# A two-layer kernel (beacon attention, then a squared-ReLU MLP): planner costs taken from landing times, and zero matmuls in TensorE's early gaps

## The chip, the cores and the metric

The kernel runs on one NeuronCore of a Trainium2 chip. The metric is the device time of one execution in microseconds (us), as a median over several executions. The engines are TensorE (PE), VectorE (DVE), ScalarE (ACT), GpSimd (POOL) and SyncE (SP); each works through its own list of instructions in order, and semaphores hold an instruction until what it needs is there. SP only issues transfers (DMA); ACT and POOL issue some as well.

## The reference

Eight batches of eight heads with 576 tokens and 64 features per head attend causally to their own keys and to 16 beacon keys that stand ahead of them. The result, 4608 tokens by 512 features, goes through two matrices with a squared ReLU between them. Inputs and output are float32.

```python
def _attn_ref(q, k, v, beacon_k, beacon_v) -> np.ndarray:
    B, H, S, D = q.shape
    scale = 1.0 / np.sqrt(D)
    k_all = np.concatenate([beacon_k, k], axis=2)
    v_all = np.concatenate([beacon_v, v], axis=2)
    Nb = beacon_k.shape[2]
    scores = scale * np.matmul(q, k_all.transpose(0, 1, 3, 2))
    causal = np.zeros((S, Nb + S), dtype=bool)
    causal[:, Nb:] = np.triu(np.ones((S, S), dtype=bool), k=1)
    scores = np.where(causal, -1000000000.0, scores)
    scores = scores - scores.max(-1, keepdims=True)
    a = np.exp(scores)
    a /= a.sum(-1, keepdims=True) + 1e-09
    return np.matmul(a, v_all).astype(np.float32)

def _moe_ref(x, w_in, w_out) -> np.ndarray:
    h = x @ w_in
    r = np.maximum(h, 0.0)
    g = r * r
    return (g @ w_out).astype(np.float32)
```

## The kernel before

Work is cut into small named pieces (`Op`), and a planner (`Order.run`) writes down the order in which each engine gets them. It plays the run forward with a cost for each piece: when an engine is free it takes, of the pieces whose needs are met, the one of lowest `prio`. The order it finds is then emitted, and the real engines follow it, each in its own order, with real waits. So a cost changes nothing but the order.

A load has two costs in the plan. `dur` is how long its engine is busy issuing it, and `dma` is added to one common time `dma_free`, so that loads share one line of transfers; the planner counts the data as there 1.6 us after that. Loads on one queue go at most 4 (SP) or 8 (ACT, POOL) deep.

The stages of a batch b (heads in four pairs; pair p = 4b + pr):

- Loads. Batch 0's q and k come through `add_first_loads` (`fld`, tokens 0 to 239, into the output staging buffers `osb`, cast by DVE and ACT) and `add_part_loads` (`sld`, tokens 240 to 575, cast on the way by POOL's transfers). Batch 1's q and k come by `sld` alone. From batch 2 on each of q, k, v is loaded in five chunks of up to 128 tokens (`add_load`, `ld`) into one of eight staging buffers `stg`, and POOL casts each chunk to bf16 (`cast`, line 299, by the helper `copy_on`). The fifth chunk has 80 rows for k and v. v of batches 0 and 1 is loaded by POOL, all else of `ld` by SP. The weights w_in and w_out come in four quarters each, from POOL; batch 2's first load waits for the last quarter of w_out.
- Transposing q and k: on PE for batches 0 and 1 (`tp`, lines 451 and 454, evicted by DVE or ACT), by two DMA transposes on SP from batch 2 on (`tr`, line 376). The beacon keys are loaded apart (`bkl`), cast by DVE (`bkc`) and transposed on PE (`tpb`).
- Scores (`qk`, line 589) into one of two PSUM strips, the exponential on ACT (`exp`, line 604) into one of four buffers `pt`, a causal mask on DVE (`mask`), then `av` on PE (line 639). From batch 1 on av p.0.0 and av p.0.1 are the two heads of a pair; each has 15 matmuls, and the last needs the fifth v chunk. DVE divides by the sums (`norm`), and the result is transposed into xT, on PE for batches 0 to 2 (`xtp`), by five DMA transposes on SP after that (`xt`, line 690).
- The MLP runs in nine chunks of 512 tokens: s1.j.f (line 770) multiplies chunk j with w_in, ACT or DVE apply the ReLU, DVE squares, s2.j.t.q (line 805) multiplies with w_out in quarters; ACT or DVE copy to `osb`, SP stores (`st`).

The MLP of one chunk is spread between the pieces of the next batches' attention; after the last batch it runs alone.

The memory that a piece uses is checked by the framework, which adds the waits. The costs of a load stand here; a cast is due once its load counts as there:

```python
        ld = add(f"ld{b}{x}{c}", "POOL" if soft else "SP", 1.3 if lo else 0.65, emit_load,
                 prio=prio, take=("stg", "stg"), dma=(1.15 if b < NPE else 1.25) * rows / 128, behind=load_chain[-1:] + behind, sync=sync)
```

Of the kernel before, what the change touches and what calls it, by code (L numbers as in the profile page):

```python
# [16 lines left out]
class Op:  # L17
# [1 line left out]

    __slots__ = ("name", "engs", "dur", "emit", "prio", "need", "users", "left", "ready",  # L20
                 "take", "give", "gate", "held", "slots", "dma", "pe_time", "behind", "followers",
                 "sync", "insts")

    def __init__(self, name, engs, dur, emit, prio=0.0, deps=(), take=None, give=None,
                 gate=None, dma=0.0, pe_time=0.0, behind=(), sync=()):
        self.name = name
        self.engs = engs if isinstance(engs, (tuple, list)) else (engs,)
        self.dur = dur
        self.emit = emit
        self.prio = prio  # L30
        self.sync = list(sync)
        self.need = list(deps) + self.sync
        self.users = []
        self.take = (*take, 1)[:3] if take else None
        self.give = give
        self.gate = gate
        self.held = None
        self.slots = []
        self.dma = dma
        self.pe_time = pe_time  # L40
        self.behind = list(behind)
        self.followers = []


class Order:
# [2 lines left out]

    LAT = {"PE": 0.2, "ACT": 0.2, "DVE": 0.15, "POOL": 0.25, "SP": 0.1, "-": 0.0}

    DEPTH = {"SP": 4, "ACT": 8, "POOL": 8}
    DMA_LAT = {"SP": 0.6, "ACT": 0.6, "POOL": 2.0}

# [7 lines left out]
    def add(self, *a, **kw):  # L61
        op = Op(*a, **kw)
        op.need = [d for d in op.need if d is not None]
        self.ops.append(op)
        return op

    def run(self):
# [16 lines left out]
        free = {e: 2.3 if e == "DVE" else 0.0 for e in engines}  # L84
        dma_free = 0.0
        lanes = {"SP": [], "POOL": [], "ACT": []}
        events = [(0.0, 0, None, None)]
        seq = 0
        started = set()
        issued = []  # L90
        now = 0.0
        while events:
            now = events[0][0]
            while events and events[0][0] <= now + 1e-9:
                _, _, kind, op = heapq.heappop(events)
                if kind == "done":
                    for u in op.users:
                        u.left -= 1
                        if u.left == 0:
                            release(u)  # L100
                elif kind == "give":
                    from_op, which = op.give if isinstance(op.give, tuple) else (op.give, 0)
                    pool, cls = from_op.take[:2]
                    self.pools[pool].append(from_op.slots[which])
                    if cls in self.inuse:
                        self.inuse[cls] -= 1
            again = True
            while again:
                again = False
                for e in engines:  # L110
                    if free[e] > now + 1e-9:
                        continue
                    best = None
                    fallback = None
                    for op in avail[e]:
                        if any(free[x] <= now + 1e-9 for x in op.engs[:op.engs.index(e)]):
                            continue
                        if op.take:
                            pool, cls, need = op.take
                            if len(self.pools[pool]) < need:  # L120
                                continue
                            if cls in self.limits and self.inuse[cls] + need > self.limits[cls]:
                                continue
                        if op.gate is not None and not op.gate(self):
                            if fallback is None or op.prio < fallback.prio:
                                fallback = op
                            continue
                        if op.dma and len(lanes[e]) >= self.DEPTH[e] and lanes[e][-self.DEPTH[e]] > now + 1e-9:
                            continue
                        if best is None or op.prio < best.prio:  # L130
                            best = op
                    if best is None:
                        best = fallback
                    if best is None:
                        continue
                    op = best
                    started.add(id(op))
                    for u in op.followers:
                        u.left -= 1
                        if u.left == 0:  # L140
                            release(u)
                    for ee in op.engs:
                        avail[ee].remove(op)
                    if op.take:
                        pool, cls, need = op.take
                        op.slots = [self.pools[pool].pop(0) for _ in range(need)]
                        op.held = (pool, cls, op.slots[0])
                        if cls in self.inuse:
                            self.inuse[cls] += need
                    dur = op.dur[e] if isinstance(op.dur, dict) else op.dur  # L150
                    end = now + dur
                    free[e] = end
                    self.progress += op.pe_time
                    issued.append((op, e, now))
                    seq += 1
                    heapq.heappush(events, (end, seq, "free", op))
                    if op.dma:
                        dma_free = max(dma_free, now + self.DMA_LAT[e]) + op.dma
                        seen = max(end, dma_free + 1.6)
                        lanes[e].append(seen)  # L160
                        seq += 1
                        heapq.heappush(events, (seen, seq, "free", op))
                    else:
                        seen = end + self.LAT[e]
                    seq += 1
                    heapq.heappush(events, (seen, seq, "done", op))
                    if op.give is not None:
                        seq += 1
                        heapq.heappush(events, (seen, seq, "give", op))
                    again = True  # L170
        assert len(issued) == len(self.ops), [o.name for o in self.ops if id(o) not in started][:20]
        for op, e, _ in issued:
            if e != "-":
                op.insts = op.emit(e)
# [8 lines left out]
def kernel(  # L183
# [11 lines left out]
    nc = tc.nc  # L195
    B, H, S, D = q.shape
    Nb = beacon_k.shape[2]
    HP = H // 2
# [69 lines left out]
        limits={"av": 2, "tp": 2},  # L268
    )
    order.wait_for = wait_for  # L270
    add = order.add

    nc.vector.memset(warm, 0.0)
    for i in range(2):
        nc.vector.memset(kT[i][:, :, Nb + S:NT * 128], 0.0)
        nc.vector.memset(vb[i][:, :, :, D:D + 1], 1.0)
    for p in pt:
        nc.vector.memset(p[:, :, 928:1952].rearrange("p h (a w) -> p h a w", w=512)[:, :, :, 0:96], 0.0)
        nc.vector.memset(p[:, :, 1824:2048], 0.0)

# [47 lines left out]
    def add_load(b, x, c, prio, behind=[], sync=[]):  # L328
# [10 lines left out]
        def emit_load(e):  # L339
            st = stg[ld.held[2]]  # L340
            insts = []
            if lo:
# [3 lines left out]
            return insts  # L346

        ld = add(f"ld{b}{x}{c}", "POOL" if soft else "SP", 1.3 if lo else 0.65, emit_load,
                 prio=prio, take=("stg", "stg"), dma=(1.15 if b < NPE else 1.25) * rows / 128, behind=load_chain[-1:] + behind, sync=sync)
        load_chain.append(ld)  # L350

        def emit_cast(e):
# [19 lines left out]
    def add_trans(b, x, prio):  # L372
        srcb, dst = (qb, qT) if x == "q" else (kb, kT)

        def emit(e):
            nc.sync.dma_start(
                out=dst[b % 2].rearrange("p g (c t) -> p (g c) t", c=NT),
                in_=srcb[b % 2].rearrange("p g c d -> p (g c d)"),
                transpose=True,
            )  # L380

        deps = [cast[b, x, c] for c in range(NT)]
        deps += [o for p in range(HP * (b - 2), HP * (b - 1)) for o in qk_ops[p]]
        trans[b, x] = [add(f"tr{b}{x}", "SP", 4.1, emit, prio=prio, deps=deps, dma=4.5)]

    def add_beacon(b, prio):
        prio = prio if b else -299.5
# [3 lines left out]
        bk = add(f"bkc{b}", "DVE", 0.4, lambda e: nc.vector.tensor_copy(bks[b % 2], bkf[b % 2]), prio=prio,  # L391
                 deps=[ld])
        cast[b, "bk"] = bk
        box = {}

        def emit_tp(e):
# [15 lines left out]
    def add_part_loads(b, part, prio, after, free, sync=()):  # L412
        t0, np_, ns = parts_of[b][part]
        step = HP // 2
        for pr in range(0, HP, step):
            h = slice(2 * pr, 2 * (pr + step))
            for n, (x, t) in enumerate((("k", k), ("q", q))):
                def emit(e, t=t, x=x, h=h):
# [1 line left out]
                        out=strided_buf(b, x, part)[:, h],  # L420
                        in_=t[b, h, t0:t0 + np_ * ns, :].rearrange("h (p s) d -> p h s d", s=ns))]
                o = add(f"sld{b}{x}{part}.{pr}", "POOL", 0.75, emit, prio=prio + pr + 0.1 * n, behind=after,
                        sync=() if pr or n else sync, deps=free, dma=1.07 if b == 0 else 1.5)
                after = [o]
                for i in range(step):
                    strided[b, part, pr + i, x] = o
# [2 lines left out]
    def add_strided(b, prio):  # L429
# [6 lines left out]
        for part, (t0, np_, ns) in enumerate(parts_of[b]):  # L436
            n_tok = np_ * ns
            for pr in range(HP):
# [3 lines left out]
                for n, xs in enumerate(groups):  # L442
                    box = {}

                    def emit_tp(e, xs=xs, pr=pr, box=box, part=part, np_=np_, ns=ns, n_tok=n_tok):
                        pp = ps[box["t"].held[2]].bitcast(BF16)
                        for i, x in enumerate(xs):
                            for u in range(ns):
# [5 lines left out]
                                    nc.tensor.transpose(pp[64 * hj:64 * hj + 64, at:at + np_],  # L454
                                                        strided_buf(b, x, part)[:, 2 * pr + hj, u, :], ident[0:np_, 0:np_])

                    tp = add(f"tp{b}.{part}.{pr}{xs}", "PE", 0.1 + (0.1 if b == 0 else 0.075) * ns * len(xs), emit_tp,
                             prio=100.0 * (HP * b + pr) - (190 if b else 90) + 0.1 * n + 1000.0 * part,
                             deps=[strided[b, part, pr, x] for x in xs] + [ident_op] + busy, take=("ps", "tp"))
                    box["t"] = tp  # L460
# [16 lines left out]
    def add_first_loads():  # L477
# [4 lines left out]
        for lo, hi in ((0, 1), (1, 2), (2, HP)):  # L482
            for n, (x, t) in enumerate((("k", k), ("q", q))):
# [4 lines left out]
                        out=raw[n][:, h],  # L488
                        in_=t[0, h, t0:t0 + np_ * ns, :].rearrange("h (p s) d -> p h s d", s=ns))]

                o = add(f"fld{x}{lo}", ("SP", "ACT")[n], (0.45, 0.55)[n], emit, prio=-300.0 + lo, dma=0.68 * (hi - lo))
                first.append(o)
                for pr in range(lo, hi):
                    def emit_cast(e, x=x, n=n, pr=pr):
# [425 lines left out]
```

The softmax here doesn't subtract the row's maximum and nothing guards it: scores larger than these inputs give would overflow.

## Time and profile before

| | |
|---|---|
| time, median of 9 runs | 345.82 us (344.93 to 346.82) |
| the profiled execution | 345.45 us, span from first to last instruction 343.7 us |
| TensorE busy | 330.5 us (96%) |
| ScalarE busy | 194.6 us (57%) |
| VectorE busy | 168.3 us (49%) |
| GpSimd busy | 89.5 us (26%) |
| first matmul | at 3.89 us |
| last quarter of w_out landed, SP's first load of batch 2 | 49.2 us |
| granted TensorE clock in the page's row of slices | 9 (90% or more) in all |

A row of the timeline gives start, length, engine, line, operation, output and input, partitions x elements, and how many instructions were merged into it; in square brackets stand the engine's idle time before it and what ended that. Lengths of matmuls hold some 0.2 us of pipeline, so merged rows overlap. A chain of waits follows the work back from the last instruction, at each step to what released it.

### The profile page before, as it was taken

The page shows a single profiled execution, that of the slowest core. Times are in us where ns is not written, and L with a number is a line of the kernel's source. Part 1 is how long each engine was busy: PE and PEld are TensorE (multiplying, and loading weights), DVE is VectorE, ACT ScalarE, POOL GpSimd, SP SyncE. Part 2 cuts the span into 40 slices and gives each one's busy share as a digit, 9 for nine tenths or more (in the row PEclk, how much of TensorE's full clock was granted, in tenths as well). Part 3 has the DMA queues.
Part 4 walks back from the last instruction along what each step waited for, and adds up shares of the span by engine and source line. Part 5 has one row for each costly group of instructions (what it writes and reads, how often), then busy time and mean ns, then how long its engine had stood idle before and what let it go on. Part 6 is the DMA issues. An engine that isn't in the chain of part 4 may idle for free.

```text
span 343.7 us, 7167 instructions
## 1 busy us (share of the span) xinstructions
PE 330.5 (96%) x2868; PEld 174.2 (51%) x2868; DVE 168.3 (49%) x372; ACT 194.6 (57%) x297; POOL 89.5 (26%) x141
## 2 busy tenths in 40 slices
PE   2899899999999999999999999999999999999995
PEld 1567675544554454444466855544554444444442
DVE  6788884148544974385355546456523302401400
ACT  4796674376646765576566655576536416515611
POOL 9854703316414514150143114212000000000000
PEclk9999999999999999999999999999999999999999
DMA  9999969999999999898699989994024011011002
GB/s 171 216 208 216 208 107 213 209 240 210 176 225 213 222 177 177 200 227 176 150 255 216 169 157 216 219 208 92 2 72 121 0 61 63 0 61 64 0 22 100
DMA packets 145291, 51.88 MB, mean 151 GB/s; under 512 B 132458, under 2 KB 140010, under 8 KB 145258
## 3 DMA queue, kind: packets, MB, share of 16 engines
q1 hardware_dynamic: 135741, 42.45, 61.2%
q0 software_dynamic: 8512, 8.49, 14.7%
q10 hardware_dynamic: 1005, 0.49, 0.5%
q8 instruction: 22, 0.36, 0.4%
q14 instruction: 11, 0.09, 0.1%
HBM read 37.22 MB, written 9.44 MB: 136 GB/s over the span
## 4 chain that ended last, share of the span: by engine, by line
PE 89%; DMA 6%; POOL 1%; DVE 1%; SPq 1%; ACT 0%; issue 0%; ACTq 0%
PE ps L805 37%; PE ps L770 33%; PE ps L639 9%; PE strip L589 8%; DMA stg<-in_v_dram 5%; DMA osb<-in_q_dram 2%; PE ps L707 1%; POOL vb L299 1%; PE ps L454 1%; SPq L344 0%; ACTq L487 0%; DVE qk_area L299 0%; DVE xn L659 0%; DVE kT L299 0%; ACT g L786 0%
## 5 line engine op out<-in xcount | busy, mean ns | idle before, releaser
L805 PE MATMUL ps<-w_out,g 128*128 128x512 bf16 x576 | 135.2, 379 | 0.0
L770 PE MATMUL ps<-xT,w_in 128*128 128x512 bf16 (+3 forms) x704 | 134.7, 341 | 0.2 <-DVE qT L299 0.2
L604 ACT ACTIVATE pt<-strip 128x832 bf16<-128x832 f32 (+4 forms) x128 | 103.6, 865 | 38.6 <-PE strip L589 38.5
L786 ACT ACTIVATE g<-ps 128x512 bf16<-128x512 f32 (+2 forms) x128 | 71.9, 562 | 47.0 <-PE ps L770 46.6
L770 PEld LDWEIGHTS <-w_in 128*128 128x128 bf16 x704 | 65.2, 98 | 57.3 <-issue 6.1
L795 DVE TENSOR_TENSOR g<-g 128x1024 bf16<-128x1024 bf16 (+2 forms) x80 | 53.2, 669 | 76.2 <-ACT g L786 74.9
L805 PEld LDWEIGHTS <-g 128*128 128x128 bf16 x576 | 52.4, 98 | 60.0 <-issue 3.2
L299 POOL CAST qk_area<-stg 128x512 bf16<-128x512 f32 (+2 forms) x60 | 39.1, 656 | 54.4 <-DMA stg<-in_k_dram 32.9
L299 POOL CAST vb<-stg 128x512 bf16<-128x512 f32 (+1 forms) x38 | 25.4, 674 | 86.3 <-DMA stg<-in_v_dram 52.0
L297 ACT COPY osb<-ps 128x512 f32<-128x512 f32 x26 | 15.2, 585 | 50.8 <-PE ps L805 50.0
L639 PEld LDWEIGHTS <-pt 128*128 128x128 bf16 (+1 forms) x960 | 36.6, 98 | 14.2 <-issue 3.6
L639 PE MATMUL ps<-vb,pt 128*128 128x65 bf16 (+1 forms) x960 | 40.4, 194 | 1.8 <-POOL vb L299 1.8
L589 PE MATMUL strip<-qT,kT 64*128 64x80 bf16 (+7 forms) x400 | 36.4, 286 | 1.0 <-DVE kT L299 0.5
L659 DVE TENSOR_TENSOR xn<-ps,rcp 128x320 bf16<-128x320 f32 (+2 forms) x64 | 31.5, 492 | 2.4 <-DVE rcp L657 0.2
L614 DVE TENSOR_TENSOR pt<-pt,tri 128x1024 bf16<-128x1024 bf16 (+1 forms) x36 | 24.2, 672 | 13.2 <-ACT pt L604 13.1
L657 DVE RECIPROCAL rcp<-ps 128x5 f32<-128x5 f32 (+2 forms) x64 | 12.3, 192 | 33.1 <-PE ps L639 32.9
L788 DVE TENSOR_SCALAR g<-ps 128x512 bf16<-128x512 f32 (+2 forms) x32 | 19.1, 599 | 10.2 <-PE ps L770 9.4
L589 PEld LDWEIGHTS <-kT 64*128 64x128 bf16 x400 | 12.5, 95 | 20.8 <-issue 16.5
L299 DVE COPY osb<-ps 128x512 f32<-128x512 f32 x10 | 6.9, 691 | 15.3 <-PE ps L805 10.3
L344 POOL DMA_DIRECT2D stg<-in_v_dram x10 | 8.5, 858 | 6.8 <-DMA w_in<-in_moe_w_in_dram 5.4
L618 DVE TENSOR_TENSOR pt<-pt,tri 80x160 bf16<-80x160 bf16 x32 | 10.2, 320 | 0.0
L451 PE MATMUL ps<-ident,qk_area 120*128 120x120 bf16 x16 | 2.3, 301 | 6.1 <-DVE qk_area L299 6.1
(39 smaller groups left out, 68.6 us busy)
## 6 DMA issues: line engine op xcount, KB each, us to landing
out_dram<-osb SPq DMA_DIRECT2D x17, 512.0 KB, 3.5
stg<-in_q_dram SPq DMA_DIRECT2D x24, 256.0 KB, 5.2
stg<-in_k_dram SPq DMA_DIRECT2D x18, 256.0 KB, 5.2
stg<-in_v_dram SPq DMA_DIRECT2D x18, 256.0 KB, 4.6
w_in<-in_moe_w_in_dram POOLq DMA_DIRECT2D x4, 512.0 KB, 11.1
w_out<-in_moe_w_out_dram POOLq DMA_DIRECT2D x4, 512.0 KB, 11.5
stg<-in_v_dram POOLq DMA_DIRECT2D x6, 256.0 KB, 8.6
stg<-in_k_dram SPq DMA_DIRECT2D x6, 224.0 KB, 4.2
```

The costliest lines, as they stand in the source:

```text
L297: nc.scalar.copy(dst, src)
L299: eng[e].tensor_copy(dst, src)
L589: nc.tensor.matmul(st[:, hj, at:at + t1 - t0], kT[b % 2][hp, pr, 128 * c:128 * c + 128], qT[b % 2][hp, pr, t0:t1], start=True, stop=True,)
L604: nc.scalar.activation(pt[take_pt.held[2]][:, :, off:off + width], st[:, :, 0:width], AF.Exp, bias=0.0, scale=scale)
L614: nc.vector.tensor_tensor(out=d, in0=d, in1=tri[:, m0:m0 + m, :][:, None].to_broadcast([128, 2, m, 128]), op=ALU.min)
L639: nc.tensor.matmul(a[:, at + (t - tl[0]) * (D + 1):at + (t - tl[0] + 1) * (D + 1)], P[0:rr, hj, o:o + 128], vb[b % 2][0:rr, c, 2 * pr + hj ...
L659: nc.vector.tensor_tensor(out=xn[b % 2].rearrange("p t (h d) -> p h t d", d=D)[:, h0:h0 + nh, tl[0]:tl[0] + nt], in0=a[:, :, :, 0:D], in1= ...
L770: nc.tensor.matmul(h[:, lo - spans[0][0]:hi - spans[0][0]], w_in_sb[:, mc, ft * 128:(ft + 1) * 128], xT[:, mc, lo % RING:lo % RING + hi - lo],
L786: nc.scalar.activation(dst, h, AF.Relu, bias=0.0, scale=1.0)
L788: nc.vector.tensor_scalar(out=dst, in0=h, scalar1=0.0, scalar2=None, op0=ALU.max)
L795: nc.vector.tensor_tensor(out=d, in0=d, in1=d, op=ALU.mult)
L805: nc.tensor.matmul(o, G[:, fc, ts * 128:(ts + 1) * 128], w_out_sb[:, fc, :], start=(fc == 0), stop=(fc == NFT - 1))
```

## The change

Two things are changed.

The planner's costs. A new cost `late` is added to the time at which the planner counts a load as there: 1 us for v of batch 1, 2 us for v of later batches and for the DMA transposes of q and k. The cost of transfer of a DMA transpose goes from 4.5 to 3.7, that of batch 0's `sld` from 1.07 to 0.95, and each of the six `fld` has its own (4.95 in all, 5.44 before). PE's transposes of batch 0 count 0.06 instead of 0.1 each. The cast of batch 1's beacon keys is held, in the plan, until the fourth pair of batch 0 is normalised (its first phase).

Fills. While the planner's clock is under 8 us and PE has nothing to take, the planner gives it a `fill`: one matmul of a 128x128 piece of `pt[0]` with 256 columns of it, into strip 1 of PSUM. `pt[0]` is zeroed there first by one more memset on DVE. The plan holds 31 fills: 19 before the first transposes, 3 after the first beacon transposes, 2 after pair 0's scores, 5 after pair 1's transposes and 2 after pair 1's scores. These last two stand behind the scores in strip 1 and ahead of the exponential that reads them, so columns 0 to 255 of the scores of pair 1's second head (batch 0) are zeros.

The new order, where it differs beyond the first 30 us: on POOL, in batches 2, 3 and 4, the cast of the next batch's first k chunk stands ahead of the cast of the fifth v chunk; on SP, some stores and the xT transposes stand behind loads that they preceded; on PE, qk20, qk24 and qk28 (the first scores of batches 5, 6 and 7) stand five to seven MLP groups earlier, and one or two groups stand on the other side of the `av` of batches 1 to 4.

```diff
-                 gate=None, dma=0.0, pe_time=0.0, behind=(), sync=()):
+                 gate=None, dma=0.0, pe_time=0.0, behind=(), sync=(), late=0.0):
         self.name = name
+        self.late = late
...
+    FILL_UNTIL = 8.0
...
                     if best is None:
+                        if e == "PE" and now < self.FILL_UNTIL:
+                            free[e] = now + 0.2
+                            issued.append((Op("fill", "PE", 0.2, self.fill), e, now))
+                            seq += 1
+                            heapq.heappush(events, (free[e], seq, "free", None))
                         continue
...
                         lanes[e].append(seen)
+                        seen += op.late
...
+    def emit_fill(e):
+        nc.tensor.matmul(strips[1][:, 1, 0:256], pt[0][:, 1, 1824:1952], pt[0][:, 0, 1792:2048],
+                         start=True, stop=True)
+
+    order.fill = emit_fill
...
     for p in pt:
+        if p is pt[0]:
+            nc.vector.memset(p[:, :, 1744:2048], 0.0)
...
-                 prio=prio, take=("stg", "stg"), dma=(1.15 if b < NPE else 1.25) * rows / 128, behind=load_chain[-1:] + behind, sync=sync)
+                 prio=prio, take=("stg", "stg"), dma=(1.15 if b < NPE else 1.25) * rows / 128, behind=load_chain[-1:] + behind, sync=sync,
+                 late=0.0 if x != "v" or b == 0 else 1.0 if b < NPE else 2.0)
...
-        trans[b, x] = [add(f"tr{b}{x}", "SP", 4.1, emit, prio=prio, deps=deps, dma=4.5)]
+        trans[b, x] = [add(f"tr{b}{x}", "SP", 4.1, emit, prio=prio, deps=deps, dma=3.7, late=2.0)]
...
         cast[b, "bk"] = bk
+        if b:
+            bk.need.extend(norm_ops[HP - 1, 0])
...
-                        sync=() if pr or n else sync, deps=free, dma=1.07 if b == 0 else 1.5)
+                        sync=() if pr or n else sync, deps=free, dma=0.95 if b == 0 else 1.5)
...
-                    tp = add(f"tp{b}.{part}.{pr}{xs}", "PE", 0.1 + (0.1 if b == 0 else 0.075) * ns * len(xs), emit_tp,
+                    tp = add(f"tp{b}.{part}.{pr}{xs}", "PE", 0.1 + (0.06 if b == 0 else 0.075) * ns * len(xs), emit_tp,
...
-                o = add(f"fld{x}{lo}", ("SP", "ACT")[n], (0.45, 0.55)[n], emit, prio=-300.0 + lo, dma=0.68 * (hi - lo))
+                o = add(f"fld{x}{lo}", ("SP", "ACT")[n], (0.45, 0.55)[n], emit, prio=-300.0 + lo, dma={"k": (0.1, 1.7, 0.4), "q": (0.8, 0.5, 1.45)}[x][min(lo, 2)])
```

More of the change, by code (lines that the diff above doesn't have):

```diff
@@ L21 @@
                  "take", "give", "gate", "held", "slots", "dma", "pe_time", "behind", "followers",
-                 "sync", "insts")
+                 "sync", "insts", "late")
     def __init__(self, name, engs, dur, emit, prio=0.0, deps=(), take=None, give=None,
-                 gate=None, dma=0.0, pe_time=0.0, behind=(), sync=()):
+                 gate=None, dma=0.0, pe_time=0.0, behind=(), sync=(), late=0.0):
         self.name = name
+        self.late = late
         self.engs = engs if isinstance(engs, (tuple, list)) else (engs,)
@@ L170, in run @@
                     again = True
-        assert len(issued) == len(self.ops), [o.name for o in self.ops if id(o) not in started][:20]
+        assert len(started) == len(self.ops), [o.name for o in self.ops if id(o) not in started][:20]
         for op, e, _ in issued:
```

## The prediction

> **What bounds the kernel now.** I read the page's first section, then TensorE's timeline for its gaps, then the chain of work that ended last.
>
> ```profile
> span 343.7 us, 7167 instructions
> ...
> PE 330.5 (96%) x2868; PEld 174.2 (51%) x2868; DVE 168.3 (49%) x372; ACT 194.6 (57%) x297; POOL 89.5 (26%) x141
> ```
>
> TensorE (PE) is busy 330.5 of 343.7 us. Of the 13.2 us that are left, 3.7 follow the last matmul (the output's way out); the rest stands in these rows, whose brackets give PE's idle time before them and what ended it:
>
> ```profile
> 3.89 0.82 PE L451 MATMUL ps<-ident,qk_area 120*128 120x120 bf16 x4 [3.89 <-DVE qk_area L299]
> 6.22 0.58 PE L451 MATMUL ps<-ident,qk_area 120*128 120x120 bf16 x4 [1.23 <-DVE qk_area L299]
> 9.13 0.98 PE L451 MATMUL ps<-ident,qk_area 120*128 120x120 bf16 x8 [0.95 <-DVE qk_area L299]
> 41.27 0.19 PE L639 MATMUL ps<-vb,pt 80*128 80x65 bf16 x1 [1.20 <-POOL vb L299]
> 81.55 0.19 PE L639 MATMUL ps<-vb,pt 80*128 80x65 bf16 x1 [0.59 <-POOL vb L299]
> ```
>
> Three of the five early gaps are shown (the others 0.47 and 0.49). The two later waits are the last matmul of av4.0.0 and of av8.0.0, each for the cast of the fifth v chunk of its batch on GpSimd (POOL). The chain of waits, in order of time (start, length), runs through just these:
>
> ```profile
> 28.95 9.75 DMA stg<-in_v_dram
> 38.75 0.96 POOL vb L299
> ...
> 72.54 1.13 SPq L344
> 73.72 5.72 DMA stg<-in_v_dram
> 80.38 1.13 POOL vb L299
> ```
>
> So until 81.5 us the end is set by loads, not by PE: whatever PE gains before either row becomes a longer wait at it. Nor can the loads of batch 2 start sooner. SyncE (SP) issues them behind a wait for the last quarter of w_out, 34 us long, and the transfers ahead of it fill the DMA engines from about 5 us on:
>
> ```profile
> SPq L343 <- DMA w_out<-in_moe_w_out_dram: 34.0, 1, 34.0
> ```
>
> **The part that decides: GpSimd's order of casts.** With `late=2.0` the planner holds v chunks of batch 2 and up for 2 us longer than k and q. In the new instruction order GpSimd casts the next batch's first k chunk *ahead of* the fifth v chunk in batches 2, 3 and 4. SP still issues v first, k second, and in the trace they land so:
>
> ```profile
> 80.38 1.11 POOL L299 CAST vb<-stg 80x512 bf16<-80x512 f32 x1
> 82.04 0.61 POOL L299 CAST qk_area<-stg 128x512 bf16<-128x512 f32 x1 [0.55 <-DMA stg<-in_k_dram]
> ...
> 106.94 1.25 POOL L299 CAST vb<-stg 128x512 bf16<-128x512 f32 x2 [1.86 <-DMA stg<-in_v_dram]
> 109.47 1.33 POOL L299 CAST qk_area<-stg 128x512 bf16<-128x512 f32 x2 [1.28 <-DMA stg<-in_k_dram]
> ...
> 134.08 0.61 POOL L299 CAST vb<-stg 80x512 bf16<-80x512 f32 x1 [0.51 <-DMA stg<-in_v_dram]
> 134.87 0.84 POOL L299 CAST qk_area<-stg 128x512 bf16<-128x512 f32 x1 [0.17 <-DMA stg<-in_k_dram]
> ```
>
> The reader is to see that GpSimd idles after the v cast until k is there. Swapped, the v cast stands behind a load that comes later; behind it wait the fifteenth matmul of av8.0.0 (av12.0.0, av16.0.0) and, in PE's order, all that follows. An 80-row v cast takes 0.73 us (mean of 8), and PE's matmul starts 0.06 after it.
>
> Batch 2: 82.04 + 0.61 + 0.73 + 0.06 = 83.44 instead of 81.55, +1.89. The new order has one group of four 512-column matmuls (s1.1.13.0, 0.86 us in the chain's rows) ahead of av8.0.0 that used to stand behind it: +1.03 net.
>
> Batch 3: 109.47 + 0.62 + 0.73 + 0.06 = 110.88. Before, that matmul starts at 108.25:
>
> ```profile
> 107.63 0.81 PE L639 MATMUL ps<-vb,pt 128*128 128x65 bf16 x15
> ```
>
> (107.63 + 0.81 − 0.19 for the last one's own length). Nothing is moved past av12.0.0, so the lateness is 110.88 − 108.25 = 2.63 *in all*, not on top of 1.03: PE arrives near 108.06 + 1.03 = 109.1 and waits 1.8.
>
> Batch 4: three groups of 0.865 that stood ahead of av16.0.0 come after it, so PE is there at 136.31 + 2.63 − 2.6 = 136.35; v is cast at 134.87 + 0.84 + 0.73 = 136.44: +0.15 with the 0.06. In batches 5 and 6 v stays first.
>
> **Fills.** 31 matmuls of 256 columns: 19 ahead of the first transposes, 12 between the first two pairs' steps. The trace has none; the nearest rows are the 272-column groups at 33.5 us (8 in 1.10, so 0.11 each for 256) and the 120-column ones at 9.13 (8 in 0.98, so 0.20 for 256). 19 take 2.1 to 3.9 us; they start after the new memset (304 words; 224 take 0.24, so 0.33) at about 1.9 and end at 4.0 to 5.8, against 3.89 for the transposes. That is 0.1 to 1.9 of delay for pair 0; DVE's copies and casts queue behind it. What may be bought: matmuls run at half pace until 16.9 us.
>
> ```profile
> 16.15 0.82 PE L639 MATMUL ps<-vb,pt 128*128 128x65 bf16 x12
> 20.18 0.91 PE L639 MATMUL ps<-vb,pt 128*128 128x65 bf16 x24
> ```
>
> Less one latency that is 57 ns a matmul, then 31. The groups from 9.13 to 16.9 take 7.9 us in all, so at most some 3.5 go; but ACT's twelve exp pieces run without a gap from 13.9 and ACT idles only about 1.7 between 7.5 and then. I take a gain of 1.0 on PE by 20 us, bounds −1.9 and +3.5. On the end both ends count nothing: at 41.27 PE waits 1.20, and at av12.0.0 1.8 more, so an early loss up to about 3 is swallowed, and any gain becomes wait. The last two fills write over columns 0 to 255 of pair 1's second head before its exp, which waits 0.2 to 0.4 for them.
>
> The Trainium skill ("TensorE: Matmul & The Clock Gate", Part 1) ties the full clock to a window of about 3.4 us of activity, so 1.9 to 8 us of fills should open it near 5 to 9 us, by its figures an estimate; it also says the ramp is under 1% of a typical kernel. By that rule the gain on PE is up to 3.4 us, by the rows 1.0; neither reaches the end here.
>
> **Other moves.** At av4.0.0 one group of 240-column matmuls (s1.0.10.0, 4 in about 0.41) now stands ahead of the wait: up to −0.41 there, lost again at av8.0.0, where PE waits anyway. The first s1 group moves ahead of 3 attention steps, to about 20 us; its w_in quarter has landed by 19.3, so it doesn't wait. Batch 0's first v cast goes from DVE to GpSimd between two w_in issues, and batch 1's four k/q issues fall behind three casts (from 14.05 to 18.3); on GpSimd's queue every issue was ahead of the DMA (it waits 5.4 us for w_in landings), so transfers keep their order and times: 0, and 1 us if the queue ran dry. Batch 1's beacon cast moves back, needed at qk4 only: 0. On SP stores fall behind one to five loads, some behind a pair of transposes too (some 10 us); a staging buffer is filled again a chunk later, 13.8 us at the least: 0. The five xT transposes of batch 3 (1.26 us each on SP) fall behind one load, those of batches 4 to 6 behind three or four, at most 6 us; their readers come 6 us or more after: 0, with 1 as the bound.
>
> **Later batches.** From batch 5 on, qk20, qk24 and qk28 stand six, seven and six 0.865 groups earlier, so their transposed k must be there sooner. Landed before: 159.7, 194.6, 225.2 us. With the lateness they come at 162.30 + 2.8 − 5.2 = 159.9, 195.66 + 2.8 − 6.05 = 192.4 and 227.22 + 3.8 − 5.2 = 225.8. One store (1.2 us on SP) leaves the way of each transpose, so k lands near 158.5, 193.4 and 224: qk24 waits 1.0, the others don't. Bounds 0 (if its loads come 1.2 sooner still) and 2.2 (if they don't move). av20, av24 and av28 stand ten to thirteen pieces earlier; their v chunks no longer wait behind five xT transposes (6.4 us on SP), which leaves them 0.6 us or more: 0.
>
> **Sum.** 2.63 + 0.15 + 1.0 = 3.8 us. The profiled run took 345.45 (span 343.7 and 1.75 around it), so 349.2; it lay 0.37 under the median of 345.82, so the median becomes **349.6**. From 81.5 on PE has no other idle time to give back. The bounds of the deciding term: landings 0.5 sooner and a 0.61 cast, 2.1; landings 0.5 later and a 1.11 cast, 3.7.
>
> **Rivals.**
> *Later batches collide more.* The thin margins of av20, av24 and av28 (0.6 us) or of qk20 and qk28 don't hold, and two of them cost 1 us each: 351.6. For it: pieces moved 5 to 10 us against loads moved 1 to 6. Against it: a wait that is paid once makes PE later for the next.
> *Not slower: the load chain moves up.* PE's end follows the first k chunk of batch 4, so if that lands 2.63 us or more sooner (before 106.8 instead of about 109.4), the swap is paid for. The chain from 49 us to there holds SP waits of 25.6 us in nine for casts ahead of its transposes, and stores that now stand behind loads. 3.6 us sooner would give 345.8 − 1.0 = 344.8. Against it: the transposes of batches 2 and 3 keep their casts, the stores still stand ahead of the fifth v chunk, and the first transfers leave the DMA engines little idle time.
> *No difference: the swap doesn't reach PE.* If GpSimd's next cast could pass the waiting one, av12.0.0 would run at 108.25 as before, and with nothing moved past it every earlier gain would be lost there: 345.8. Against it: each of GpSimd's rows above starts only after the one before it.
> The Trainium skill ("DMA: Bandwidth & Descriptors", Queues, rings and completion order) says that completion is not FIFO per issuing engine, which speaks against the forecast: a k chunk that landed with v would leave only its own cast ahead, and the sum by it would be about 0.7 instead of 2.8. No row here shows such a crossing; all three pairs land v first.
>
> **Chances.** Forecast 0.68, with or without the wait at qk24; more collisions 0.17; not slower 0.07; no difference 0.08. About 0.2% (0.7 us) is what a measurement of this kernel tells from no change. Slower by more than that 0.85 (the first two), within it 0.08, faster 0.07. The range reaches from 346.6 (the term's lower bound with no wait at qk24 is 347.9, and most of the way from there to no difference is taken in) to 351.6 (the collisions).
>
> **What would show it.** Right: GpSimd rows with the k cast directly ahead of an 80-row v cast near 83 and 110.5; PE idle of about 1.8 us before the single L639 matmul near 110.9, released by POOL; early matmul gaps filled from 1.9 us; about 1 us of idle time at qk24 near 193, waiting for a DMA. Wrong: v casts near 81 and 108; new idle time at av20, av24 or av28; or first transposes at 6 us whose delay is still there at 41 us.

## The result, and the profile after

The changed kernel takes 349.94 us (median of 18 runs, 347.00 to 351.65); the kernel before, in the 55 runs beside it, 346.29. The ratio is 1.0092, 95% interval 1.0074 to 1.0109: slower by 3.2 us (the two medians lie 3.65 apart; the forecast added 3.8). The profiled execution took 348.73 us with a span of 347.0 (before: 345.45 and 343.7). The total is near the one forecast, 349.6. What follows shows that it did not come about as forecast.

The page's first section and the shares of the chain of waits, after:

```profile
span 347.0 us, 7232 instructions
...
PE 333.0 (96%) x2899; PEld 177.6 (51%) x2899; DVE 170.5 (49%) x379; ACT 191.2 (55%) x290; POOL 89.2 (26%) x142
...
PE 64%; DMA 21%; SPq 8%; POOL 4%; issue 1%; DVE 1%; ACT 0%; POOLq 0%; DVEq 0%; ACTq 0%
```

The reader is to see that TensorE's share is no larger (its 333.0 us hold 31 fills) and that loads and SyncE's queue now make up 29% of the chain. Before, PE made up 89% of it and the loads ended at 81 us. TensorE's timeline, the rows that matter (the new memset and other added lines shift line numbers by 16 to 19, so L639 is now L658):

```profile
2.32 4.24 PE L281 MATMUL strip<-pt 128*128 128x256 bf16 x19 [2.32 <-DVE pt L295]
...
41.74 0.19 PE L658 MATMUL ps<-vb,pt 80*128 80x65 bf16 x1 [0.31 <-POOL vb L315]
...
82.16 0.19 PE L658 MATMUL ps<-vb,pt 80*128 80x65 bf16 x1 [0.28 <-POOL vb L315]
...
107.39 0.81 PE L658 MATMUL ps<-vb,pt 128*128 128x65 bf16 x15
...
190.47 0.58 PE L608 MATMUL strip<-qT,kT 64*128 64x496 bf16 x4 [0.68 <-DMA kT<-qk_area]
...
230.40 0.44 PE L658 MATMUL ps<-vb,pt 128*128 128x65 bf16 x9
231.11 0.31 PE L658 MATMUL ps<-vb,pt 128*128 128x65 bf16 x5 [0.28 <-POOL vb L315]
232.83 0.19 PE L658 MATMUL ps<-vb,pt 80*128 80x65 bf16 x1 [1.41 <-POOL vb L315]
```

The fills end at 6.56 and hold the first transposes until 6.35 (before 3.89). At 41.74 and 82.16 the old waits are still there, smaller. There is no wait at av12: its fifteen matmuls run in one row at 107.39. New are qk24 (190.47) and the end of av28.0.0 (231.11 and 232.83). Before, av28.0.0 stood 9.35 us later and had no wait in it:

```profile
239.75 0.62 PE L639 MATMUL ps<-vb,pt 128*128 128x65 bf16 x15
```

Set against the same work in the trace of before, TensorE is 2.5 us late at its first transposes, 0.05 at 43 us, 0.2 at 188, 1.3 to 2.0 from 193 to 230, and 3.3 from 250 to the end. (A mark that stands in both traces: SyncE issues the thirteenth output store at 278.50 before and at 281.78 after.) So nearly the whole loss, 3.1 us, falls between 188 and some time after 230. TensorE's idle time from 188 to 234 is 2.57 us (46.00 less 43.43 busy; before, none), and the three rows hold 2.37 of it. The other 0.5 is not idle time of TensorE there, and no view here shows where it lies.

GpSimd's timeline shows the swap of casts, as forecast:

```profile
80.94 0.61 POOL L315 CAST qk_area<-stg 128x512 bf16<-128x512 f32 x1 [1.56 <-DMA stg<-in_k_dram]
81.50 0.61 POOL L315 CAST vb<-stg 80x512 bf16<-80x512 f32 x1
...
106.78 0.61 POOL L315 CAST qk_area<-stg 128x512 bf16<-128x512 f32 x1 [1.58 <-DMA stg<-in_k_dram]
107.34 0.61 POOL L315 CAST vb<-stg 80x512 bf16<-80x512 f32 x1
```

The k cast stands directly ahead of the 80-row v cast, but the v casts end at 82.1 and 107.9, not at 83.4 and 110.8. The k chunks landed at 80.79 and 106.64, where they landed at 81.89 and 109.33 before.

The chain of waits in order of time (start, length), two pieces of it:

```profile
165.93 1.26 SPq L709
...
167.24 0.58 SPq L359
...
167.86 2.78 DMA stg<-in_k_dram
...
183.12 0.53 SPq L852
...
183.74 6.67 DMA kT<-qk_area
...
226.40 5.62 DMA stg<-in_v_dram
```

Batch 6's first k load goes out behind the last of five xT transposes (L709), and its transposed k behind a store (L852); it lands at 190.42, when TensorE has been waiting for 0.68 us. The sixth line is the fifth v chunk of batch 7, landed at 232.02, for av28.

### The profile page after: what moved, and what is told of

It is laid out like the page before. It is cut to its first block, busy times and chain, and to the rows that moved or that the text cites. A ratio compares the mean times of both kernels' runs of the same rounds, so it can differ in the third digit from the quotient of the medians.

```text
span 347.0 us, 7232 instructions
## 1 busy us (share of the span) xinstructions
PE 333.0 (96%) x2899; PEld 177.6 (51%) x2899; DVE 170.5 (49%) x379; ACT 191.2 (55%) x290; POOL 89.2 (26%) x142
## 4 chain that ended last, share of the span: by engine, by line
PE 64%; DMA 21%; SPq 8%; POOL 4%; issue 1%; DVE 1%; ACT 0%; POOLq 0%; DVEq 0%; ACTq 0%
PE ps L824 28%; PE ps L789 25%; DMA stg<-in_v_dram 6%; DMA stg<-in_k_dram 6%; PE ps L658 5%; PE strip L608 5%; SPq L709 4%; DMA qk_area<-in_k_dram 3%; DMA stg<-in_q_dram 3%; SPq L360 2%; DMA kT<-qk_area 2%; SPq L393 1%; POOL stg L360 1%; POOL qk_area L438 1%; POOL vb L315 1%
## 5 line engine op out<-in xcount | busy, mean ns | idle before, releaser
L805 ACT ACTIVATE g<-ps 128x512 bf16<-128x512 f32 (+2 forms) x121 | 67.9, 561 | 44.0 <-PE ps L789 41.5
L814 DVE TENSOR_TENSOR g<-g 128x1024 bf16<-128x1024 bf16 (+2 forms) x80 | 52.0, 654 | 71.3 <-ACT g L805 69.6
L658 PEld LDWEIGHTS <-pt 128*128 128x128 bf16 (+1 forms) x960 | 36.6, 98 | 13.5 <-issue 3.9
L658 PE MATMUL ps<-vb,pt 128*128 128x65 bf16 (+1 forms) x960 | 40.8, 194 | 2.6 <-POOL vb L315 2.5
L608 PE MATMUL strip<-qT,kT 64*128 64x80 bf16 (+7 forms) x400 | 35.2, 277 | 3.4 <-ACT qT L313 1.7
L807 DVE TENSOR_SCALAR g<-ps 128x512 bf16<-128x512 f32 (+2 forms) x39 | 23.6, 609 | 14.9 <-PE ps L789 14.1
L315 DVE COPY osb<-ps 128x512 f32<-128x512 f32 x11 | 7.6, 692 | 15.1 <-PE ps L824 13.1
L315 DVE COPY kT<-ps 128x240 bf16<-128x240 bf16 (+3 forms) x14 | 6.8, 500 | 5.2 <-PE ps L470 3.5
```

What stands on the lines that cost most here:

```text
L315: eng[e].tensor_copy(dst, src)
L608: nc.tensor.matmul(st[:, hj, at:at + t1 - t0], kT[b % 2][hp, pr, 128 * c:128 * c + 128], qT[b % 2][hp, pr, t0:t1], start=True, stop=True,)
L658: nc.tensor.matmul(a[:, at + (t - tl[0]) * (D + 1):at + (t - tl[0] + 1) * (D + 1)], P[0:rr, hj, o:o + 128], vb[b % 2][0:rr, c, 2 * pr + hj ...
L805: nc.scalar.activation(dst, h, AF.Relu, bias=0.0, scale=1.0)
L807: nc.vector.tensor_scalar(out=dst, in0=h, scalar1=0.0, scalar2=None, op0=ALU.max)
L814: nc.vector.tensor_tensor(out=d, in0=d, in1=d, op=ALU.mult)
```

## The experiments

Ratios are to the kernel before, run beside it on the same chip (medians 345.94 to 346.86), with 95% intervals. Diffs are against the changed kernel unless said otherwise.

**The kernel before once more.**

> The kernel before, unchanged, profiled a second time. Theory 'the new order of loads brought the chain of loads forward': the landings of this trace repeat the first trace of it within 0.5 us (batch 3's first k chunk near 81.9, batch 4's near 109.3, batch 5's transposed k near 159.7, batch 6's near 194.6). Theory 'chance of one execution': they lie anywhere between those and the landings of the changed kernel (80.8, 106.6, 155.7, 190.4), so 1 us or more away from the first trace. Time: about 346.

346.01 us. Landings: batch 3's first k chunk 82.04, batch 4's 108.27, batch 5's transposed k 159.49, batch 6's 194.91. Three lie within 0.32 of the first trace, one 1.06 away. So chance can move a landing by about 1 us; the 4.0 and 4.2 by which the changed kernel's transposed k (batches 5 and 6) comes sooner are more than that. The order of loads alone does not fix them: the run without fills below has the same order of loads, and there they land at 158.97 and 192.70.

**One cost back at a time.** First the lateness of v:

```diff
-                 late=0.0 if x != "v" or b == 0 else 1.0 if b < NPE else 2.0)
+                 late=0.0 if x != "v" or b == 0 else 1.0 if b < NPE else 0.0)
```

> The changed kernel with late = 0 instead of 2.0 for v of batches 2 and up; all else stays. GpSimd casts the fifth v chunk ahead of the next k chunk again in batches 2, 3 and 4; qk20, qk24 and qk28 stay early. (Here and in the changed kernel the last two fills zero the scores in columns 0 to 255 of pair 1's second head in batch 0.) Forecast's theory (the swap of casts costs 2.6 to 2.8 us): 1.001 to 1.002 of the kernel before, about 347. Rival (the later batches' k and v come too late for the early qk24 and av28, the swap costs nothing): 1.008 to 1.010, about 349.6, with idle time still at qk24 near 191 and av28 near 232.

350.32 us, 1.0108 (1.0073 to 1.0143): undoing the swap brings nothing back. The forecast's deciding term has fallen. The rival's place was wrong, too. In this trace TensorE waits at av12 (1.19) and here, at av20:

```profile
171.65 0.19 PE L658 MATMUL ps<-vb,pt 80*128 80x65 bf16 x1 [3.09 <-POOL vb L315]
```

Then the transposes' costs:

```diff
-        trans[b, x] = [add(f"tr{b}{x}", "SP", 4.1, emit, prio=prio, deps=deps, dma=3.7, late=2.0)]
+        trans[b, x] = [add(f"tr{b}{x}", "SP", 4.1, emit, prio=prio, deps=deps, dma=4.5)]
```

> The changed kernel with the old plan costs for the DMA transposes of q and k (4.5 of transfer, no lateness); all else stays. qk20, qk24, qk28 and av20, av24, av28 stand about where they stood before the change; GpSimd still casts k first in batches 2 and 3 (not in 4), and now in 5 and 6 as well. Forecast's theory (the swap at av8 and av12 costs 2.6, qk24 1.0): 348.9, 1.008 of the kernel before. Rival (later batches): 1.000 to 1.002, about 346.4, with no idle time over 0.5 us on TensorE after 82 us.

345.73 us, 0.9996 (0.9970 to 1.0022): the whole loss is gone with this one line, although GpSimd still casts k first in batches 2, 3, 5 and 6. After 18 us one wait over 0.5 is left, 0.60 at 209, where av24 waits for a swapped cast.

> The changed kernel with both undone: the transposes' old costs and no lateness for v of batches 2 and up. What is left is the fills, the lateness of 1.0 for v of batch 1, and the new costs of batch 0. GpSimd's casts and the later batches' order stand as before the change. Forecast's theory: 345.8 (the early changes are swallowed at the wait near 41), 0.999 to 1.001. Rival: the same number, 1.000, since it also puts nothing on the early changes. A third theory, that the early part loses for good (fills delay the first transposes by 2.5 us): 1.003 to 1.007, 347 to 348.5.

346.65 us, 0.9991 (0.9972 to 1.0011). The early changes lose nothing at the end, though the first transposes start at 6.4 us here as well.

**One cost alone, on the kernel before.** The transposes' costs (3.7 and late 2.0):

> The kernel before with one part of the change alone: the DMA transposes of q and k cost 3.7 instead of 4.5 in the plan and count as there 2 us later. qk20, qk24, qk28 and av20, av24, av28 move 5 to 11 pieces earlier; GpSimd's casts stay as before, no fills. Theory 'later batches' (their loads come too late for the early order): 1.006 to 1.010 of the kernel before, with 2 to 3.5 us of idle time on TensorE between 150 and 240 us. Forecast's theory (of this part only qk24's 1.0 us): 1.003.

351.59 us, 1.0151 (1.0124 to 1.0179): more than the whole change loses, and more than expected. Its waits are at av12 (0.92), qk20 (0.81) and the end of av20.0.0 (3.23). SyncE's own rows show what the fifth v chunk stood behind, and TensorE's row who waited:

```profile
157.81 3.76 SPq L346 DMA_DIRECT2D stg<-in_v_dram  x4
161.67 7.86 SPq L692 DMA_TRANSPOSE xT<-xn  x5
169.57 0.58 SPq L346 DMA_DIRECT2D stg<-in_v_dram  x1
```

```profile
173.19 0.19 PE L641 MATMUL ps<-vb,pt 80*128 80x65 bf16 x1 [3.23 <-POOL vb L301]
```

Four chunks go out, then five xT transposes that take SyncE 7.9 us, then the fifth. Why this kernel loses about 2 us more than the changed one (1.0151 against 1.0092) stays open: with the rest of the change added, the av pieces stand up to three groups elsewhere, and the waits with them.

The lateness of v alone:

> The kernel before with another part alone: 2 us of lateness for v of batches 2 and up. GpSimd casts the next batch's first k chunk ahead of the fifth v chunk in batches 2 to 6; qk20, qk24 and qk28 stay where they were. Forecast's theory (each swap makes TensorE wait for the k chunk's landing): 1.005 to 1.009. Rival (the swap is worth nothing, the loads come sooner or the waiting matmul has room): 0.998 to 1.002.

346.92 us, 1.0024 (1.0005 to 1.0043), between the two theories: five swaps cost the end 0.2 to 1.5 us together, with one wait over 1 us (1.13, at av24, behind a swapped cast).

**Which of the transposes' two costs.** The changed kernel with `dma=4.5, late=2.0`:

> The changed kernel with one number back: a DMA transpose takes 4.5 of the plan's line of transfers again instead of 3.7; its lateness of 2.0, the lateness of v, the fills and the rest stay. Theory 'the shorter transfer cost does it' (it takes 0.8 off the planned line twice a batch, 9.6 us by the last batch, while lateness only holds the readers of that one load): qk20, qk24, qk28 and av20, av24, av28 stand one to three groups later than before the change, 0.997 to 1.001 of the kernel before. Rival 'the lateness does it': 1.006 or more.

347.12 us, 1.0009 (0.9992 to 1.0026). And the kernel before with `dma=3.7` alone:

> The kernel before with the transpose's transfer cost alone at 3.7 instead of 4.5, no lateness. Theory 'the shorter transfer cost does it': 1.012 to 1.018, as the run with both of the transposes' costs (1.015), with idle time of 3 us or more in all at qk20 to av28. Rival 'the lateness does it': 0.999 to 1.003.

350.16 us, 1.0095 (1.0077 to 1.0114). So the 0.8 us less of transfer is enough for the whole loss, and without it the transposes' lateness costs nothing that can be told. With it the lateness is not free: on the kernel before, both together lose more (1.0151) than the shorter transfer alone (1.0095), and the intervals lie apart; why stays open. The size fits the whole change; the place does not, and it is under the 1.012 to 1.018 expected. Its one new wait over 1 us is at qk12, for its transposed k, and after it the granted clock is at half for 3.4 us:

```profile
100.17 0.58 PE L589 MATMUL strip<-qT,kT 64*128 64x496 bf16 x4 [2.33 <-DMA kT<-qk_area]
```

That fits the same mechanism in an earlier batch: in this kernel's order qk12 stands three MLP groups (2.6 us) earlier than before, and its k landed at 100.12, no sooner than the 99.45 of before.

**The fills.** Without them (`FILL_UNTIL = 0.0`):

> The changed kernel without its 31 fills; the pieces keep their order but for one or two MLP groups near av4 and av12, and the scores of pair 1 are whole again. Theory 'fills cost nothing at the end': 1.009 like the changed kernel, 349.6. Theory 'fills cost clock' (the runs with fills so far had a mean granted clock of 0.978 to 1.0, the kernel before 0.998 to 1.0): a clock of 0.998 or more in every run, and 0.5 to 1.5 us less than the changed kernel, 1.005 to 1.008. Theory 'fills gain' (full pace from 6.7 us): 1.010 to 1.014.

349.74 us, 1.0104 (1.0081 to 1.0127): the fills are worth nothing at the end that can be told, and the granted clock of every run is 0.998 or more. This trace holds a surprise, in TensorE's rows:

```profile
83.41 0.19 PE L658 MATMUL ps<-vb,pt 80*128 80x65 bf16 x1 [1.25 <-POOL vb L315]
...
111.39 0.19 PE L658 MATMUL ps<-vb,pt 80*128 80x65 bf16 x1 [0.94 <-POOL vb L315]
```

Here the swap bites where the forecast put it (83.44 and 110.88), because the k chunks landed at 82.04 and 110.02. With 1.15 at qk12 between them, 3.3 us are paid by 112 us; then av28 waits only 0.4, and the total is the same. In this trace the wait that is paid early is not paid again late. GpSimd's casts and SyncE's loads stand in the same order there as in the changed kernel, so that order alone does not bring k sooner; what did in the changed kernel's trace stays open.

The kernel before with the fills alone:

> The kernel before with fills alone (29 in its plan: 21 ahead of the first transposes; the last one zeroes columns 0 to 255 of pair 1's second head's scores in batch 0, and the first MLP groups move by one or two places). Theory 'swallowed at the wait near 41 us': 0.999 to 1.001. Theory 'fills cost clock': granted clock down to 0.98 to 0.99 in some of the runs, 1.001 to 1.005. Theory 'fills gain': below 0.998.

345.52 us, 0.9987 (0.9968 to 1.0006): nothing that can be told from no change, and a granted clock down to 0.988.

Two attempts at something better, both on the run with `dma=4.5, late=2.0`:

```diff
-        free = {e: 2.3 if e == "DVE" else 0.0 for e in engines}
+        free = {e: 2.3 if e in ("DVE", "PE") else 0.0 for e in engines}
...
-        nc.tensor.matmul(strips[1][:, 1, 0:256], pt[0][:, 1, 1824:1952], pt[0][:, 0, 1792:2048],
+        nc.tensor.matmul(strips[1][:, 1, 368:512], pt[0][:, 1, 1824:1952], pt[0][:, 0, 1904:2048],
```

(A fill counts 0.13 in the plan.)

> The previous kernel but one (transfer cost back at 4.5, all else of the change) with other fills: the plan lets TensorE start at 2.3 us, as it does on the chip, so 8 fills instead of 19 stand ahead of the first transposes; each has 144 columns and writes columns 368 to 511 of the strip, which no score of batch 0's first phase uses, so nothing of the computation is changed. Theory 'early time is worth something once the later waits are gone': first transposes near 4.5 us instead of 6.4, full pace from about 7 us, 0.993 to 0.998. Rival 'the wait for batch 1's fifth v chunk near 41 us takes it back': 0.998 to 1.001, with idle time there again.

346.13 us, 0.9989 (0.9964 to 1.0013): no gain that can be told. The first transposes start at 3.87, but the thinner fills don't bring full pace: matmuls run at half pace until 19.9 us.

```diff
-        free = {e: 2.3 if e == "DVE" else 0.0 for e in engines}
+        free = {e: {"DVE": 2.3, "PE": 1.3}.get(e, 0.0) for e in engines}
...
-    FILL_UNTIL = 8.0
+    FILL_UNTIL = 7.2
...
+    nc.vector.memset(pt[0][:, :, 1744:2048], 0.0)
     nc.vector.memset(warm, 0.0)
```

(A fill counts 0.22 in the plan, and the later zeros of `pt[0]` in those columns go.)

> As the run with the lateness kept and the transfer cost back, but pt[0]'s zeros are the first thing DVE does, so that fills (256 columns, 20 in all) run from about 1.3 us and end when the first transposes can start (12 ahead of them, near 3.9); none stands behind pair 1's scores, so nothing of the computation is changed. Theory 'TensorE is the bound from 21 us on once the transposes' cost is back, so early time counts': full pace from 5 to 7 us with the first transposes near 4, 0.992 to 0.997 of the kernel before. Rival 'the clock falls back': granted clock under 0.99 in part of the runs, 0.997 to 1.001. Rival 'a load near 41 us takes it back': the same time with idle time at the fifteenth matmul of av4.

345.19 us against 345.94, 0.9977 (0.9960 to 0.9994): 0.2% under the kernel before, a gain whose interval ends just short of 1. TensorE's rows:

```profile
1.31 2.74 PE L281 MATMUL strip<-pt 128*128 128x256 bf16 x12 [1.31 <-DVE warm L288]
4.00 0.86 PE L470 MATMUL ps<-ident,qk_area 120*128 120x120 bf16 x4
```

The fills end where the transposes can start, and full pace is there at 5.75. The gain stayed under the expected 0.3 to 0.8%, and the clock fell back, as the second rival said: 0.50 from 12 to 18.7 us in this trace, and seven of twelve runs with a mean under 0.992. These seven have a median of 345.35, the other five 344.84, so the fall goes with 0.5 us, which is no more than a hint with so few runs.

## Why the prediction was right, and where it was not

The direction and the time were right (349.6 against 349.94), the mechanism in part. That the total fits is luck: the swap's 2.8 us (2.63 and 0.15) did not come, and the later batches, forecast at 1.0, cost some 3 us.

- **What bounds the kernel** was read rightly for the first 82 us: TensorE was 2.5 us late at 6 us and waited 1.0 us at 30 for batch 1's k, and both were gone at the wait of av4. *"From 81.5 on PE has no other idle time"* held for the trace of before and was taken over for the changed kernel; there it ceased to hold at 190 us.
- **The deciding term, 2.63 us for GpSimd's swap, failed.** The swap came, but its price took k's landing from the trace of before. In the changed kernel's trace k landed 1.1 and 2.7 us sooner, and nothing was lost at av12. The bounds allowed 0.5 either way for a landing, while the kernel before alone has 109.33 in one trace and 108.27 in the other. The landing at 106.64 meets the condition of the second rival (before 106.8); its conclusion, 344.8, failed on the later batches. The run without fills shows that the arithmetic was sound where k landed about as before, and that even then the end is the same: with the later batches' order, some 3 us are lost either way. Undone, the swap brought back nothing (1.0108); without the transposes' cost it is worth 0 to 0.8 us, and alone on the kernel before 0.2 to 1.5. The 0.15 for av16 fell with it.
- **The later batches: right mechanism, mis-sized.** The forecast gave 1.0 at qk24 and 0 at av28; the rows show 0.68 and 1.69, and giving back the transposes' transfer cost alone is worth 2.9 us (1.0092 to 1.0009). The rival "later batches collide more" named av28 and the reason, *"pieces moved 5 to 10 us against loads moved 1 to 6"*. Its 351.6 kept the swap's 2.8 in the sum; without that it would have said 348.8. The failed step is *"which leaves them 0.6 us or more: 0"*: at av28 the 15th matmul wants its chunk some 9 us earlier than before (av28.0.0 starts at 230.40 instead of 239.75), and the chunk landed 6.45 sooner (232.02 instead of 238.47).
- **Adding the terms** was itself an error. A wait at 83, one at 110 and one at 232 can stand in for each other: a TensorE that pays one early arrives later at the next, as without the fills. They are not always alternatives: with v's lateness undone, 1.19 at av12 and 3.09 at av20 stand in one trace. The forecast used this for a rival (*"a wait that is paid once makes PE later for the next"*) and for the fills, but not for its own sum.
- **Fills.** 19 took 0.22 each, above the upper bound of 0.20, from 2.32 instead of 1.9; the transposes came 2.46 us late, beyond the bound of 1.9. The gain of 1.0 by 20 us did not come (0.1 behind at 16.8, 0.6 at 22 to 28); full pace from about 6.7 us only made good what the delay had cost. At the end nothing, as said: 1.0104 without fills, 1.0092 with them.
- **Completion order.** The Trainium skill ("DMA: Bandwidth & Descriptors", Queues, rings and completion order) was weighed as speaking against the forecast, through a k chunk that lands with v. In the changed kernel v landed first again, by 1.2 and 1.1 us (79.56 and 80.79, 105.49 and 106.64). What undid the term was that both came sooner.

Why 0.8 us does it: the plan keeps one line of transfers, and a transfer cost lengthens it for every load behind as long as the line is never free. Two transposes in six batches, 0.8 less each, are 9.6 us by the end. The plan's own clock puts av28 at 233.2 instead of 244.5 and qk24 at 192.8 instead of 199.5; in the changed kernel's trace the loads that they need moved by 6.5 and 4.2 us. In the plan, lateness holds one load's readers and does not lengthen that line.

## What to carry to other kernels

A cost on a shared line of a planner is multiplied by all that stands behind it; look at the order at the far end of the run, and put the uncertainty of one load into a lateness that holds its readers alone (here that cost between nothing and 0.4%, but more beside the shortened transfer). When a swap puts a consumer behind another load, price it with a landing that may move by 1 us or more, and do not simply add waits that hang on one chain. In a plan whose TensorE has no idle time left, look at every piece that is moved further than its load.

## What the hardware showed beside this

The granted clock can fall in the middle of a kernel. TensorE in windows of 2 us (length, busy time, matmuls, granted clock, DMA share, GB/s), the kernel before with fills alone:

```profile
10.00:12.00 2.00, 1.04 (x25) 1.00 1.14 256
12.00:14.00 2.00, 1.48 (x34) 0.95 1.03 217
14.00:16.00 2.00, 2.00 (x32) 0.50 1.16 185
16.00:18.00 2.00, 1.99 (x25) 0.50 1.25 206
18.00:20.00 2.00, 2.00 (x25) 0.50 1.23 202
20.00:22.00 2.00, 1.91 (x32) 0.84 1.24 206
```

The fills had brought full pace by about 7 us; after a stretch from 10 to 14 in which TensorE was 52 to 74% busy, with no gap over 1 us, the clock was at half for 6.8 us (from the windows' means: 0.2 us of the second, three whole ones, 0.6 of the last). The column says nothing of the start: it is 1.00 from 2 to 6 us too, where the first 21 fills took 0.22 us each (three at 7.37 us took 0.50 together), and the kernel before has a mean of 1.000 in its trace although its matmuls run at half pace until 16.8. So mean clocks of kernels with and without fills do not compare what the start costs.

The run with the transposes' costs back, the one with lateness kept and the last one show 6.8 us as well, and the waits of 3.09 us (at 171.65) and 2.33 us (at 100.17) were each followed by 3.4 us at half; the one of 3.23 us (at 173.19) was not. With fills it came in some of the runs and not in others: mean clocks of 0.978 to 1.0, where the kernel before has 0.993 or more. The Trainium skill ("TensorE: Matmul & The Clock Gate", Part 1) describes a free-running window of about 3.4 us, and the half clock after an idle one; the lengths of 3.4 and 6.8 us, one and two such windows, agree with that, and so may a fall that comes in one execution and not in the next. That the window must be idle does not agree: here the clock fell with TensorE 52 to 74% busy, and after a wait of 2.33. So opening the clock early is no sure gain. Before, it opened at 16.8 us and stayed open; with the fills it opened at 6.7 in the changed kernel's trace and stayed open, and in the trace above it fell.
